# Attention and a feed-forward layer on one core: casts by two outer rows, w_out behind V of batch 1, matmuls in the set-up, and the global rows' store ahead of the last blocks

## The chip, the core and the metric

The kernel runs on one core of one Trainium2 chip. Time is device time in microseconds (us) of one launch of the kernel on that core. Five engines work at once: TensorE (PE; its loading of weights is listed as PEld), VectorE (DVE), ScalarE (ACT), GpSimd (POOL) and SyncE (SP). POOL and SP also issue transfers; a queue's name with a q behind it (POOLq, SPq) marks that in the rows of the timeline. Transfers are carried by 16 DMA engines, which all queues share.

## What is computed

```python
# attention: B, H, S, D = 8, 8, 576, 64; 8 global tokens
scores = (q @ k.T) / sqrt(D)
mask = (abs(pos[:, None] - pos[None, :]) <= 32) | is_global[:, None] | is_global[None, :]
x = softmax(where(mask, scores, -1e9)) @ v          # then (B*S, H*D) = 4608 x 512
# feed-forward
h = x @ w_in                                        # 512 x 2048
out = (h + sin(alpha * h)**2 / (alpha + 1e-9)) @ w_out   # 2048 x 512
```

All inputs are float32; the kernel's matmuls take bf16.

## The kernel before

**Stages.** The 8 batches go through the core one after the other, in two stages. `attention(b)` (L892 to L1026; `attention_first`, about L780 to L890, for batch 0) computes 576 tokens of 8 heads, two heads (`hp`) at a time: scores within windows (L929), the exponential on ACT (L938), the mask on DVE (L939), the products with V and with ones (L967), the reciprocal through a logarithm and an exponential on ACT (L771, L778), and the normalised result xT on DVE (L985). `gemm1(b)` (L1108 to L1165) multiplies xT by w_in in 16 groups `nt` of 128 columns (L1124) and makes H from each by a sine (L1154), a square (on ACT L1157 or DVE L1159) and one DVE operation (L1160). `gemm2(b)` (L1167 to L1190) multiplies H by w_out, in blocks of 128 tokens with 16 matmuls of 128x512 each (L1172), copies the result out of PSUM (L1182, the last block in two halves by ACT and DVE, L1180) and stores it (L1189, SP). It is a generator: `fill(n)` (L1216) takes the next n of its matmuls from a waiting list, so that they lie between the steps of the attention after it (after two heads each, by `FIRST` and `SECOND`; `NEAR` and `MIDST` at its end) and of gemm1 (`PER_GROUP`, `GROUP_LATE` in gemm1(1), `GROUP_LAST` in gemm1(7)). Rows of the 8 global tokens stand in 64 columns of their own; `gemm2_globals` (L1192 to L1211) multiplies those at the end of the kernel and scatters them into the output by POOL (L1208).

**How keys, queries and values come in.** For batches 1 to 7, POOL's queue casts k, q and v of a batch to bf16 from DRAM to DRAM (`cast_qk`, L332, buffers kd and qd; `cast_v`, L340, buffer vd; two buffers of each). SP then issues the transposing transfers kd to kt and qd to qt (`turn_qk`, L345), DVE copies these into the operands KX or KD and QX (`place`, L357 for queries, L364 for keys, eight copies a batch), and SP loads vd into VX or VD (`load_v`, L418), with the global rows of V beside it (`load_vg`, L422). For batch 0 the loads are direct (V at L397, by POOL). w_in comes in four parts of 512 columns (`load_w_in`, L430) and w_out in four parts (`load_w_out`, L436), cast by POOL's queue as well.

**What sets the order.** Every queue works in the order of the program. POOL's queue is held back by `pace` (L1241): a copy of one element that waits until the tile it reads is there, behind which the next transfers stand. In attention(0), POOL issues kd and qd of batch 1, waits by `pace` for kt of batch 1, and then issues parts 2 and 3 of w_in, vd of batch 1 and the four parts of w_out. In gemm1(0) at nt = 10 SP issues the global rows of V of batch 1; after gemm1(0) POOL issues kd and qd of batch 2. Ahead of gemm1(1) it waits by `pace` for qt of batch 2, and issues vd of batch 2 and kd, qd, vd of batch 3. From attention(2) on, `pace` waits for xT of the batch at its third pair of heads, and kd, qd, vd of the batch two further on follow. kt and qt of batch 2 are turned in attention(1), those of later batches after the gemm1 two batches earlier. The eight copies of `place` stand in gemm1(0) and gemm1(1) for batches 1 and 2 (nt 10 to 13), and in the attention before from batch 3 on: `places_at` puts two ahead of the first heads, one after the second pair, three after the third and two after the fifth step.

**The end.** gemm1(7) is followed by the blocks of gemm2(7) with the sums and squares of a check of the inputs' size (`square_x`, `square_w`, `judge_sums`, `judge`, L1043 to L1099) between them, then gemm2_globals. The verdict is read (L1314) and a branch (L1315) leads to a general path, which isn't taken here.

Of the kernel before, what the change touches and what calls it, by code (L numbers as in the profile page):

```python
# [10 lines left out]
ALU = mybir.AluOpType  # L11
AF = mybir.ActivationFunctionType
DT = mybir.dt
# [3 lines left out]
P = 128  # L17
# [232 lines left out]
def kernel(  # L250
# [65 lines left out]
    VG0 = main.tile([NG * B, D], DT.bfloat16, name="VG0")  # L316
    seen = main.tile([1, 1], DT.bfloat16, name="seen")
    girow = main.tile([1, NG], DT.int64, name="girow")
# [12 lines left out]
    def cast_qk(b):  # L331

        for src, name in ((k, "kd"), (q, "qd")):
            cast[b, name] = dramp.tile([P, H * S * D // P], DT.bfloat16, name=name)
            nc.gpsimd.dma_start(
                out=cast[b, name][:], in_=src[b].rearrange("h s d -> (h s d)").rearrange("(p f) -> p f", p=P)
            )

    def cast_v(b):

        cast[b, "vd"] = dramp.tile([S, H, D], DT.bfloat16, name="vd")
        nc.gpsimd.dma_start(out=cast[b, "vd"][:], in_=v[b].rearrange("h s d -> s h d"))

    def turn_qk(b):
# [304 lines left out]
    def place_global_queries(t, copy):  # L649
        for y in range(2):  # L650
# [246 lines left out]
    def attention(b, beside):  # L897
# [82 lines left out]
        def inverse(hp):  # L980
            Rs[hp] = inverted(Ls[hp])
# [124 lines left out]
    def gemm1(b):  # L1106
# [23 lines left out]
        for nt in range(NT):  # L1130
# [34 lines left out]


    def gemm2(b):  # L1167
        lo, hi = (0, 4) if b % 2 == 0 else (4, 9)
        for blk in range(lo, hi):
            ops = zo[(blk + b // 2) % 2]  # L1170
            for nt in range(NT):
                nc.tensor.matmul(  # L1172
                    out=ops[:], lhsT=H2[:, nt, blk * P : (blk + 1) * P], rhs=w_out[:, nt, :],
                    start=(nt == 0), stop=(nt == NT - 1),
                )
                yield True
            osb = osbp.tile([P, DM], DT.float32, name="osb")
            if b == B - 1 and blk == hi - 1:
                for e, copy in enumerate((nc.scalar.copy, nc.vector.tensor_copy)):
                    copy(out=osb[:, e * DM // 2 : (e + 1) * DM // 2], in_=ops[:, e * DM // 2 : (e + 1) * DM // 2])  # L1180
            else:
                nc.scalar.copy(out=osb[:], in_=ops[:])  # L1182

            c = blk * P
            while c < (blk + 1) * P:
                z = min((c // QTR + 1) * QTR, (blk + 1) * P)
                run, u = c // QTR, c % QTR
                t0 = (b // 2) * 2 * S + (run // 2) * HALF + run % 2 + 2 * u
                nc.sync.dma_start(  # L1189
                    out=out[t0 : t0 + 2 * (z - c) - 1 : 2, :], in_=osb[c - blk * P : z - blk * P, :]  # L1190
                )
                c = z  # L1192

# [45 lines left out]
    def pace(src):  # L1239

        nc.gpsimd.tensor_copy(out=seen[:], in_=src)  # L1241

    def phase_a(b_att, b_moe):
        def beside(at):

            if b_moe is None:
                if at == 0:
# [4 lines left out]
                    cast_v(1)  # L1252
                    load_w_out()
                    gather(v, gv)
# [27 lines left out]
    phase_a(0, None)  # L1282
    for b in range(B):
        if b == 1:
            pace(turned[2][0][0:1, 0:1])
            cast_v(2)
            cast_qk(3)
            cast_v(3)
# [6 lines left out]
        if b + 1 < B:  # L1295
# [16 lines left out]
    mctx.close()  # L1312

    sure = nc.values_load(verdict[0:1, 0:1], min_val=0, max_val=P)  # L1314
    with tc.If(sure < P):  # L1315
        general_path(tc, q, k, v, global_idx, out, w_in, w_out, alphaT, recipT)
# [30 lines left out]
```

## Time and profile before

| what | us |
|---|---|
| runs of the kernel before | 383.4, 383.32, 378.85 |
| their median | 383.32 |
| the profiled execution | 384.38 |
| its span, first to last instruction | 382.7 |
| set-up and attention(0), to | 31.4 |
| gemm1(0) | 31.4 to 54.5 |
| attention(1) | 54.5 to 82.4 |
| gemm1(1) | 82.4 to 107.0 |
| attention(2) | 107.0 to 126 |
| gemm1(2) | 126 to 147.8 |
| from then on, a batch about | 39 |
| gemm1(7) | 321 to 346 |

The profiled execution is one run with a hardware trace; its durations are what the prediction's sums are made of. Stages overlap at their edges, since matmuls of gemm2 lie in both. A row of the timeline has the start, the duration, the engine and line, the operation with what it writes and reads, a count, and in brackets how long the engine had been idle before it and which instruction ended that. A row of the waits has the engine, what it was about to write and its line, what it waited for, then the total, the number of waits and the longest. A row by windows has the window, its length, the busy time and count of PE, PEld, DVE, ACT and POOL, the granted TensorE clock as a share of full speed, the DMA share and GB/s. A row of a queue's transfers has the packets, the MB and the share of 16 engines' time that its packets took. A row of DMA issues has the buffers, the queue, the count, the KB of each and the median us from issue to landing.

### The profile page before, as it was taken

The numbers are of one execution on the slowest core, as the hardware profiler recorded it, in microseconds if no ns is written. First come the engines' busy times: TensorE is split into PE (matmuls) and PEld (weight loads), VectorE is DVE, ScalarE is ACT, GpSimd is POOL, SyncE is SP. The second block draws the span as 40 slices with busy tenths as digits, with TensorE's granted clock in tenths as the row PEclk, the third lists the DMA queues.
The fourth block names the chain that finished last, engine by engine and source line by source line (L and its number), as shares of the span: only waits on it lengthen the run. The fifth ranks groups of instructions, "written<-read, shape, count | busy, mean of one in ns | idle before, by whom it ended". The sixth has DMA issues, their size and how long they took to land. (4 is left out here: it accounts for less than half of the span.)

```text
span 382.7 us, 10443 instructions
## 1 busy us (share of the span) xinstructions
PE 323.6 (85%) x4222; PEld 206.1 (54%) x4280; DVE 275.5 (72%) x539; ACT 288.9 (75%) x425; POOL 55.1 (14%) x78
## 2 busy tenths in 40 slices
PE   2678753699988998899899989998998998899990
PEld 2566532356645664566556655665466655554440
DVE  6966897156969687967796788778877885889400
ACT  7879794278877888879887987898888886889110
POOL 7941730014004000400030002100000000000001
PEclk9999995599999999999999999999999999999996
DMA  7999999179994991395849693977232020002221
GB/s 121 117 162 170 184 207 224 27 153 153 203 196 80 208 183 30 69 189 100 149 81 163 119 153 86 146 155 123 59 93 51 0 58 32 3 0 83 64 75 49
DMA packets 91393, 43.23 MB, mean 113 GB/s; under 512 B 76394, under 2 KB 85994, under 8 KB 90890
## 3 DMA queue, kind: packets, MB, share of 16 engines
q0 software_dynamic: 44208, 18.52, 39.9%
q1 hardware_dynamic: 47130, 23.97, 30.2%
q8 instruction: 35, 0.57, 0.6%
q14 instruction: 20, 0.16, 0.1%
HBM read 41.97 MB, written 21.95 MB: 167 GB/s over the span
## 5 line engine op out<-in xcount | busy, mean ns | idle before, releaser
L1172 PE MATMUL zo<-w_out,H 128*128 128x512 bf16 x518 | 137.5, 382 | 4.6 <-issue 3.6
L1124 PEld LDWEIGHTS <-w_in 128*128 128x128 bf16 x1024 | 99.2, 98 | 53.0 <-issue 18.7
L1172 PEld LDWEIGHTS <-H 128*128 128x128 bf16 x576 | 51.0, 98 | 45.3 <-issue 0.7
L938 ACT ACTIVATE E<-ring 128x720 bf16<-128x720 f32 x56 | 43.3, 773 | 28.8 <-PE ring L929 28.8
L1124 PE MATMUL zn<-xT,w_in 128*128 128x288 bf16 (+1 forms) x384 | 57.0, 287 | 6.1 <-DVE H L1160 4.1
L1124 PE MATMUL zr<-xT,w_in 128*128 128x288 bf16 x320 | 47.7, 287 | 3.3 <-DVE H L1160 2.9
L1124 PE MATMUL zd<-xT,w_in 128*128 128x288 bf16 x320 | 46.3, 287 | 1.9 <-DMA w_in<-in_moe_w_in_dram 1.3
L1160 DVE SCALAR_TENSOR_TENSOR H<-s,recipT,zn 128x576 bf16<-128x576 bf16 (+1 forms) x48 | 39.4, 822 | 10.7 <-ACT s L1157 7.3
L1154 ACT ACTIVATE sb<-zn,alphaT 128x576 bf16<-128x576 f32 (+1 forms) x48 | 35.7, 743 | 14.6 <-PE zn L1124 13.5
L1157 ACT ACTIVATE s<-sb 128x576 bf16<-128x576 bf16 (+1 forms) x62 | 42.7, 689 | 2.0
L1159 DVE TENSOR_TENSOR s<-sb 128x576 bf16<-128x576 bf16 (+1 forms) x66 | 30.9, 468 | 14.2 <-ACT sb L1154 13.1
L939 DVE TENSOR_TENSOR E<-E,MASKT 128x720 bf16<-128x720 bf16 x56 | 29.2, 529 | 11.6 <-ACT E L938 11.1
L1160 DVE SCALAR_TENSOR_TENSOR H<-s,recipT,zd 128x576 bf16<-128x576 bf16 (+1 forms) x40 | 32.9, 822 | 6.4 <-ACT s L1157 4.3
L1160 DVE SCALAR_TENSOR_TENSOR H<-s,recipT,zr 128x576 bf16<-128x576 bf16 (+1 forms) x40 | 32.9, 822 | 5.9 <-ACT s L1157 3.4
L1154 ACT ACTIVATE sb<-zd,alphaT 128x576 bf16<-128x576 f32 (+1 forms) x40 | 29.6, 739 | 5.9 <-PE zd L1124 5.9
L1154 ACT ACTIVATE sb<-zr,alphaT 128x576 bf16<-128x576 f32 (+1 forms) x40 | 29.6, 741 | 3.5 <-PE zr L1124 3.4
L1182 ACT COPY osb<-zo 128x512 f32<-128x512 f32 x35 | 20.4, 582 | 14.2 <-PE zo L1172 14.1
L778 ACT ACTIVATE R<-L,shift 128x576 f32<-128x576 f32 x32 | 24.8, 774 | 0.6
L985 DVE TENSOR_TENSOR xT<-zn,R 128x576 bf16<-128x576 f32 x21 | 15.8, 754 | 8.8 <-PE zn L967 6.0
L1241 POOL COPY seen<-xT 1x1 bf16<-1x1 bf16 x4 | 1.9, 480 | 134.7 <-DVE GN L755 134.7
L1208 POOL DMA_INDIRECT out_dram<-osb,grow x1 | 1.0, 979 | 135.7 <-SPq L1315 135.7
L929 PEld LDWEIGHTS <-KX 64*64 64x64 bf16 x448 | 9.0, 111 | 20.9 <-issue 19.2
(169 smaller groups left out, 373.5 us busy)
## 6 DMA issues: line engine op xcount, KB each, us to landing
kd<-in_k_dram POOLq DMA_DIRECT2D x7, 576.0 KB, 6.5
qd<-in_q_dram POOLq DMA_DIRECT2D x7, 576.0 KB, 10.1
vd<-in_v_dram POOLq DMA_DIRECT2D x7, 576.0 KB, 15.4
VX<-vd SPq DMA_DIRECT2D x16, 168.0 KB
w_in<-in_moe_w_in_dram POOLq DMA_DIRECT2D x4, 512.0 KB, 5.8
w_out<-in_moe_w_out_dram POOLq DMA_DIRECT2D x4, 512.0 KB, 16.4
out_dram<-osb SPq DMA_DIRECT2D x8, 256.0 KB
VD<-vd SPq DMA_DIRECT2D x12, 168.0 KB
```

The lines of the kernel that those rows point to most:

```text
L778: nc.scalar.activation(out=R[:], in_=L[:], func=AF.Exp, scale=-1.0, bias=shift[:, 0:1])
L929: nc.tensor.matmul(out=zs[half * D : (half + 1) * D, t, 0 : G3 * WCOL].rearrange("p (m x c) -> p m x c", x=2, c=60)[:, m % G3, :, c0:c1], ...
L938: nc.scalar.activation(out=Eg, in_=zs[:, :, 0 : G3 * WCOL], func=AF.Exp, scale=scale)
L939: nc.vector.tensor_tensor(out=Eg, in0=Eg, in1=MASKT[:, None, G3 * g : G3 * (g + 1), :].rearrange("p o m c -> p o (m c)").to_broadcast([P, ...
L985: nc.vector.tensor_tensor(out=xT[:, hp, 0:S].rearrange("p (k m c) -> p k m c", k=4, c=KT), in0=tokens(nd(hp, 0)), in1=Rs[hp][:], op=ALU.mult,)
L1124: nc.tensor.matmul(out=h_part, lhsT=w_in[:, c, nt * P : (nt + 1) * P], rhs=xT[:, c, lo:hi], start=(c == 0), stop=(c == CT - 1), skip_group ...
L1154: nc.scalar.activation(out=sb[:, 0:W], in_=h, func=AF.Sin, scale=alphaT[:, nt : nt + 1])
L1157: nc.scalar.activation(out=s2[:, 0:W], in_=sb[:, 0:W], func=AF.Square)
L1159: nc.vector.tensor_tensor(out=s2[:, 0:W], in0=sb[:, 0:W], in1=sb[:, 0:W], op=ALU.mult)
L1160: nc.vector.scalar_tensor_tensor(out=H2[:, nt, r0 : r0 + W], in0=s2[:, 0:W], scalar=recipT[:, nt : nt + 1], in1=h, op0=ALU.mult, op1=ALU.add,)
L1172: nc.tensor.matmul(out=ops[:], lhsT=H2[:, nt, blk * P : (blk + 1) * P], rhs=w_out[:, nt, :], start=(nt == 0), stop=(nt == NT - 1),)
L1182: nc.scalar.copy(out=osb[:], in_=ops[:])
```

## The change

1. `cast_qk` views source and destination as two outer rows ("p (a c) -> a p c" with a = 2), each of 128 runs of 1,152 elements, where both were one contiguous list before.
2. `load_w_out` moves from attention(0) to gemm1(0), nt = 10, behind `load_vg(1)` and a new `pace` that reads 48 partitions of the second half of VX, the values of batch 1.
3. Twice seven matmuls whose result isn't used (`warm`) stand around the turning of keys and queries in the set-up.
4. At the end of an attention, `fill(NEAR)` stands ahead of the numerators of the last but one pair of heads.
5. `GROUP_LAST` takes 3 and then 13 times 1 matmul of gemm2(6) in gemm1(7), where it took 4 in all; 14 are left over there.
6. `gemm2_globals` and its scatter stand ahead of gemm2(7). For that, H of the global tokens of batch 7 is copied to its columns by eight POOL copies (`put_globals`, columns read from registers that `load_columns` fills at b = 2).
7. The last block of gemm2 is computed in two halves of 256 columns, each with its own copy by ACT and its own store.
8. The copies of `place` for batch 3 move to after the third pair (two) and after the fifth step (six) of attention(2).
9. The branch at the end has the general path as the one that is jumped to.

```diff
         for src, name in ((k, "kd"), (q, "qd")):
-            nc.gpsimd.dma_start(
-                out=cast[b, name][:], in_=src[b].rearrange("h s d -> (h s d)").rearrange("(p f) -> p f", p=P)
-            )
+            runs = [
+                t.rearrange("p (a c) -> a p c", a=2)
+                for t in (cast[b, name][:], src[b].rearrange("h s d -> (h s d)").rearrange("(p f) -> p f", p=P))
+            ]
+            nc.gpsimd.dma_start(out=runs[0], in_=runs[1])
...
+    warm(zo[0], 7)
     turn_part(1, 0, views([zn[:, n, :] for n in range(2)]))
...
     turn_part(0, 0, views([zd[:, n, :] for n in range(2)]))
+    warm(zo[0], 7)
...
         inverse(last - 1)
+        fill(NEAR)
         numerators(last - 1)
-        fill(NEAR)
...
                 load_vg(1)
+                pace(VX[1][D : D + KT, 0, 0, 0:1])
+                load_w_out()
...
+    def put_globals():
+        for j, c in enumerate(columns_of):
+            g = 2 * S + j * B + B - 1
+            nc.gpsimd.tensor_copy(out=H2[:, :, bass.ds(c, 1)], in_=H2[:, :, g : g + 1])
...
+            parts = 2 if (b, blk) == (B - 1, hi - 1) else 1
+            for part in range(parts):
+                cols = slice(part * DM // parts, (part + 1) * DM // parts)
+                if part:
+                    ops = zd[:, 1]
...
+                nc.scalar.copy(out=osb[:, cols], in_=ops[:, cols])
+                store(b, blk, osb, cols)
...
-    GROUP_LAST = (0, 0, 2) + 2 * (0, 0, 0, 1) + 5 * (0,)
+    GROUP_LAST = (0, 0, 3) + 13 * (1,)
...
-        share = {-1: (0, 2), 1: (2, 3), 2: (3, 6), 4: (6, 8)}
+        share = {2: (0, 2), 4: (2, 8)} if b_att == 2 else {-1: (0, 2), 1: (2, 3), 2: (3, 6), 4: (6, 8)}
...
                     load_w_in((2, 3))
                     cast_v(1)
-                    load_w_out()
...
-    waiting.append(gemm2(B - 1))
+    put_globals()
     square_x(B - 1, 0)
     square_x(B - 1, 1)
-    for c in range(CT):
+    square_w(0)
+    fill(NT)
+    square_w(1)
+    fill(4 * NT)
+    gemm2_globals()
+    judge_sums()
+    waiting.append(gemm2(B - 1))
+    for c in (2, 3):
         square_w(c)
         fill(NT)
-        if c == 1:
-            judge_sums()
     judge()
     fill(2 * NT * NT)
-    gemm2_globals()
...
-    with tc.If(sure < P):
+    with tc.If(sure < P, preferred_fallthrough_block=False):
```

On POOL, from the casts of batch 1 in attention(0) to those of batch 2 behind gemm1(0), the kernel before has these rows (a transfer's row has the shape of its destination, outermost dimension first; `seen` is what `pace` writes, KX, QX and VGb belong to batch 1):

```order
L335 DMA kd<-in_k_dram 32x9216
L335 DMA qd<-in_q_dram 32x9216
L1241 COPY seen<-kt 1x1
L430 DMA w_in<-in_moe_w_in_dram 128x4x512 x2
L342 DMA vd<-in_v_dram 4608x1x64
L436 DMA w_out<-in_moe_w_out_dram 128x4x512 x4
L1260 COPY MASKT<-MASK 64x720 x2
L719 CAST VGb<-H_97 64x512
L377 COPY KX_94<-kTg 128x48x8
L380 COPY QX_96<-qTg 128x4x7x4 x2
L335 DMA kd<-in_k_dram 32x9216
L335 DMA qd<-in_q_dram 32x9216
```

The changed kernel has these at the same place:

```order
L340 DMA kd<-in_k_dram 2x128x1152
L340 DMA qd<-in_q_dram 2x128x1152
L349 COPY seen<-kt 1x1
L437 DMA w_in<-in_moe_w_in_dram 128x4x512 x2
L345 DMA vd<-in_v_dram 4608x1x64
L1298 COPY MASKT<-MASK 64x720 x2
L728 CAST VGb<-H_97 64x512
L384 COPY KX_94<-kTg 128x48x8
L387 COPY QX_96<-qTg 128x4x7x4 x2
L349 COPY seen<-VX_93 48x1
L443 DMA w_out<-in_moe_w_out_dram 128x4x512 x4
L340 DMA kd<-in_k_dram 2x128x1152
```

w_out has moved from between vd of batch 1 and the copies of the mask to behind a second copy into `seen`, and stands directly ahead of kd and qd of batch 2; the casts' shape has changed.

On DVE, in attention(2), the copies of batch 3 (KX from kt, QX from qt) stand among the masks of the scores (E), the sums over the global tokens (GD, GN) and the results xT. Before, the piece from the first of them to the one behind the third pair of heads reads:

```order
L364 COPY KX_94<-kt 64x48x24 x2
L939 TENSOR_TENSOR E<-E,MASKT 128x2x360 x2
L1053 TENSOR_TENSOR SQ<-xT 128x4x576
L939 TENSOR_TENSOR E<-E,MASKT 128x2x360 x2
L755 TENSOR_REDUCE GD<-zd 128x2x4
```

And after the change, the piece with the first two of them:

```order
L948 TENSOR_TENSOR E<-E,MASKT 128x2x360
L764 TENSOR_REDUCE GD<-zd 128x2x4
L371 COPY KX_94<-kt 64x48x24 x2
L948 TENSOR_TENSOR E<-E,MASKT 128x2x360
L994 TENSOR_TENSOR xT<-zn,R 128x576
```

The two copies have moved from ahead of the first mask of attention(2) to behind the second GD, where a single copy of KX stood before; the six others follow together behind the last GN of that attention.

On POOL, at the end of the program, the kernel before has these rows (the last casts, the scatter, the reading of the verdict):

```order
L1241 COPY seen<-xT 1x1
L335 DMA kd<-in_k_dram 32x9216
L335 DMA qd<-in_q_dram 32x9216
L342 DMA vd<-in_v_dram 4608x1x64
L1208 DMA out_dram<-osb,grow 4608x512
L1314 TENSOR_LOAD verdict
L1315 COMPARE_AND_BRANCH
```

The changed kernel's end, from the last of the eight copies on:

```order
L1205 ISA
L1205 COPY H_97<-H_97 128x16
L1251 DMA out_dram<-osb,grow 4608x512
L1358 TENSOR_LOAD verdict
L1359 COMPARE_AND_BRANCH
```

The scatter now stands behind eight copies of H to H (128 partitions, 16 elements) and is followed by the same reading of the verdict; in the program it comes ahead of gemm2(7).

More of the change, by code (lines that the diff above doesn't have):

```diff
@@ L316 @@
     VG0 = main.tile([NG * B, D], DT.bfloat16, name="VG0")
-    seen = main.tile([1, 1], DT.bfloat16, name="seen")
+    seen = main.tile([P, 1], DT.bfloat16, name="seen")
+    gcol = main.tile([1, NG], DT.int32, name="gcol")
     girow = main.tile([1, NG], DT.int64, name="girow")
@@ L342, in cast_v, with pace @@
         nc.gpsimd.dma_start(out=cast[b, "vd"][:], in_=v[b].rearrange("h s d -> s h d"))
+    def pace(src):
+        nc.gpsimd.tensor_copy(out=seen[0 : src.shape[0]], in_=src)
     def turn_qk(b):
@@ L1170, in gemm2, with store @@
             ops = zo[(blk + b // 2) % 2]
[L1171 to L1176, printed above, removed]
-            osb = osbp.tile([P, DM], DT.float32, name="osb")
[L1178 to L1192, printed above, removed]
+            osb = osbp.tile([P, DM], DT.float32, name="osb")
+            parts = 2 if (b, blk) == (B - 1, hi - 1) else 1
[3 more added lines that the diff above has]
+                    ops = zd[:, 1]
+                for nt in range(NT):
+                    nc.tensor.matmul(
+                        out=ops[:, cols], lhsT=H2[:, nt, blk * P : (blk + 1) * P], rhs=w_out[:, nt, cols],
+                        start=(nt == 0), stop=(nt == NT - 1), skip_group_check=True,
+                    )
+                    yield True
+                nc.scalar.copy(out=osb[:, cols], in_=ops[:, cols])
+                store(b, blk, osb, cols)
+    def store(b, blk, osb, cols):
+        c = blk * P
+        while c < (blk + 1) * P:
+            z = min((c // QTR + 1) * QTR, (blk + 1) * P)
+            run, u = c // QTR, c % QTR
+            t0 = (b // 2) * 2 * S + (run // 2) * HALF + run % 2 + 2 * u
+            nc.sync.dma_start(
+                out=out[t0 : t0 + 2 * (z - c) - 1 : 2, cols], in_=osb[c - blk * P : z - blk * P, cols]
+            )
+            c = z
     def gemm2_globals():
```

23 lines of the change are left out of this document (21 added, 2 removed).

## The prediction, on record before the changed kernel ran

> **What bounds the kernel now.** I read the header of the page and its clock row first, then the waits by engine, the timeline of the first 120 us, the transfers of a few windows, and the tail.
>
> ```profile
> PE 323.6 (85%) x4222; PEld 206.1 (54%) x4280; DVE 275.5 (72%) x539; ACT 288.9 (75%) x425; POOL 55.1 (14%) x78
> PEclk9999995599999999999999999999999999999996
> 60.00:70.00 10.00, 2.18 (x44) 1.10 (x36) 5.49 (x16) 2.75 (x4) 0.00 (x0) 0.50 0.80 172
> 70.00:80.00 10.00, 8.84 (x195) 5.10 (x198) 3.86 (x10) 4.89 (x8) 0.00 (x0) 0.68 0.42 75
> PE zn L967 <- DMA VX<-VGb: 7.2, 2, 4.8
> PE zd L1124 <- DMA w_in<-in_moe_w_in_dram: 1.3, 1, 1.3
> ```
>
> TensorE is the busiest engine (85%) and no single wait is large. One place in the middle is weak: around 60 to 80 us PE is nearly empty, and the granted clock, 0.9 or more elsewhere, is 0.50 and 0.68 (the last two numbers but two of the window rows). The wait that ends there is for V of batch 1: 7.2 us in two pieces. The other wait, for the second half of w_in, is only 1.3 us, and it is on this row that the change bears hardest. The timeline shows the chain of POOL's queue, of SP's queue and of PE behind both (start, us, what, and in brackets the idle time before):
>
> ```profile
> 23.15 0.55 POOL L335 DMA_DIRECT2D kd<-in_k_dram  x1
> 36.65 0.18 POOL L1241 COPY seen<-kt 1x1 bf16<-1x1 bf16 x1 [12.44 <-DMA kt<-kd]
> 36.88 1.54 POOL L430 DMA_DIRECT2D w_in<-in_moe_w_in_dram  x2
> 38.41 2.26 POOL L342 DMA_DIRECT2D vd<-in_v_dram  x1
> 40.12 3.53 POOL L436 DMA_DIRECT2D w_out<-in_moe_w_out_dram  x4
> 29.60 4.68 SPq L348 DMA_TRANSPOSE kt<-kd  x1
> 51.60 1.63 SPq L418 DMA_DIRECT2D VX<-vd  x4
> 42.85 1.15 PE L1124 MATMUL zd<-xT,w_in 128*128 128x288 bf16 x8 [1.33 <-DMA w_in<-in_moe_w_in_dram]
> 67.89 0.28 PE L967 MATMUL zn<-E,VX 56*64 56x88 bf16 x2 [4.82 <-DMA VX<-VGb]
> 70.56 0.78 PE L967 MATMUL zn<-E,VX 56*64 56x88 bf16 x26 [2.39 <-DMA VX<-VGb]
> ```
>
> The reader is to see a chain without slack: cast of the keys, transpose kt, the paced POOL copy, w_in, PE at 42.85. Whatever the cast takes longer, PE gets late w_in.
>
> **The casts.** Each cast was one list of 32 rows of 9,216 elements; now its outermost dimension is 2, with 128 runs of 1,152 inside. The whole question is over how many of the 16 DMA engines two outer rows are spread.
>
> ```profile
> q0 software_dynamic: 81, 0.90, 74.5%
> q0 software_dynamic: 681, 0.68, 73.6%
> q0 software_dynamic: 44208, 18.52, 39.9%
> VD<-in_v_dram POOLq DMA_DIRECT2D x16, 36.0 KB, 4.9
> ```
>
> The first row is the window 26.4 to 32.1 us, where nearly all bytes are those of the casts: 0.745 x 16 x 5.7 = 67.9 us of engine time for 0.90 MB. Its long packets have 18,432 bytes, and 0.90 MB is 49 of them: 1.386 us for one, so 32 x 1.386 = 44.4 us for a cast, 2.8 us if 16 engines share it, 22.2 us on two. The second row is the window 36.9 to 43 us, whose packets have 1 KB: 0.736 x 16 x 6.1 / 681 = 0.105 us each. A run of 1,152 bf16 has 2,304 bytes. On the line between the two rows it takes 0.202 us, and a cast 256 x 0.202 / 2 = 25.7 us on two engines; at the rate of the 1 KB packets it would be 30 us. I take 25.7 with ends 22.2 and 30.
>
> Two engines or sixteen? The third row (the whole page) lets the packets be counted. Transfers of POOL's queue have, by their shapes, 41,824 runs of data, and 53 transfers with 16 closing writes each give 848: 42,672. The row has 44,208, which is 1,536 or 16 x 96 more. There are exactly 16 transfers whose outer dimension isn't a multiple of 16: the loads of V (fourth row), 24 rows of 12 runs. 96 is 4 x 24: as if 12 engines took two rows (24 runs) each, and 4 idle ones wrote 24 empty entries each. So the spread goes by the outer dimension (12 divides 24) and not by all runs (288 divides by 16). Two rows then give two engines. The casts' own rows show only an outer dimension of 32 and say nothing of fewer, so an even split stays a rival. The Trainium skill, page "DMA: Bandwidth & Descriptors", section "Rules for kernel authors", speaks against this change: an outermost dimension of fewer than 16 confines a transfer to at most that many engines. By that rule the sum below holds; by the even spread that the casts' rows show it would be the first rival's. No run so far shows a transfer with two rows.
>
> **Costs, step by step.** I follow the sum against the profiled execution: 384.38 us for a span of 382.7, 1.1 us over the median of 383.32 (runs 378.85 to 383.4).
>
> *First cast, +23.9 (20.4 to 28.2).* kt(1) comes 25.7 − 2.8 = 22.9 us later, POOL's copy behind it and w_in too; PE waits at nt = 8 of gemm1(0), where it is 1.3 us late already, so nothing hides it. Behind so long a wait I add 1 us for matmuls at half clock (8.84 us of PE work at 0.68 in the window above lost about 2.8 us; this wait is followed by less). SP's queue has only stores of no hurry behind kt.
>
> *V of batch 1 and w_out, −8.5 (−10 to −7.2).* w_out's four transfers no longer stand in the rings ahead of the V loads; vd goes right behind w_in. The two waits of 4.82 and 2.39 us go, and part of the slow clock (1.3 us of the 2.8). w_out now waits on POOL for V: V landed is about 75, w_out issued 76 to 80 and landed by 96. It is first used at the end of attention(1), which the first cast pushes back as well, so I cost that at nothing here.
>
> *Second casts, +12 (5 to 18).* kd(2) and qd(2), issued ahead of V until now, stand behind w_out's packets on their engines.
>
> ```profile
> 75.18 2.21 SPq L348 DMA_TRANSPOSE kt<-kd  x1
> 99.18 0.92 DVE L364 COPY KD<-kt 64x1152 bf16<-64x1152 bf16 x2
> 83.97 0.18 POOL L1241 COPY seen<-qt 1x1 bf16<-1x1 bf16 x1 [30.65 <-DMA qt<-qd]
> 86.69 1.04 POOL L335 DMA_DIRECT2D kd<-in_k_dram  x1
> 103.44 5.32 SPq L348 DMA_TRANSPOSE kt<-kd  x1
> 111.68 0.92 DVE L364 COPY KX<-kt 64x1152 bf16<-64x1152 bf16 x2 [3.29 <-DMA kt<-kd]
> 119.99 0.46 DVE L364 COPY KX<-kt 64x1152 bf16<-64x1152 bf16 x1
> q0 software_dynamic: 4134, 0.53, 140.7%
> q0 software_dynamic: 939, 1.29, 106.2%
> ```
>
> They start when w_out is through, about 96.5, land at 122, and kt(2) is turned at 126.7 (4.7 us, as kt(1)). The copy at 99.18 wants it at 99.18 + 23.9 − 8.5 = 114.6: 12 us. The ends are a w_out that lands 7 us earlier or 6 later.
>
> *Third casts, +24 (14 to 30).* POOL's copy at 83.97 waits for qt(2), now turned at 128.5. vd(2) and kd(3) are queued behind it: the last two rows are the windows 86 to 91.9 us, in which POOL's rings moved nothing but vd's short runs, and 91.9 to 98.7 us, with kd's and qd's bytes. So kd starts 8 us after the copy, now runs from 136.5 to 162, and kt(3) is there at 167 (5.32 us). The copies of batch 3 that stood at 111.68 now stand where the row of 119.99 does, ahead of which go 3.29 us of waiting and 1.37 us of copies: they want kt(3) at 115.3 + 27.4 (the sum so far) = 143. The move takes the 3.29 us away only if kt(3) is on time.
>
> *Batches 4 to 7, +10 (0 to 25).*
>
> ```profile
> 159.24 0.72 POOL L335 DMA_DIRECT2D kd<-in_k_dram  x1
> 183.55 3.06 SPq L348 DMA_TRANSPOSE kt<-kd  x1
> 190.14 0.92 DVE L364 COPY KX<-kt 64x1152 bf16<-64x1152 bf16 x2 [1.48 <-DMA kt<-kd]
> ```
>
> From issue to the first use are 188.7 − 159.2 = 29.5 us. The cast needs 1.4 us to start, 25.7 to run, and the transposes 5: 32, or 2.5 us too late, four times. With 22.2 it fits; with 30 it is 6 a batch.
>
> *Tail, −4 (−5 to −1).*
>
> ```profile
> 372.06 1.94 PE L1200 MATMUL zd<-w_out,H 128*64 128x256 bf16 x32
> 372.21 0.37 ACT L1180 COPY osb<-zo 128x256 f32<-128x256 f32 x1 [2.87 <-PE zo L1172]
> 374.08 0.37 ACT L1207 COPY osb<-zd 64x256 f32<-64x256 f32 x1 [1.50 <-PE zd L1200]
> 376.59 0.98 POOL L1208 DMA_INDIRECT out_dram<-osb,grow x1 [135.74 <-SPq L1315]
> SPq L1342 <- DMA out_dram<-osb,grow: 5.3, 1, 5.3
> ```
>
> The last product was that of the global rows: 1.94 us of matmuls, two copies, a scatter issued at 376.59 and 5.3 us of waiting for it. Done ahead of gemm2(7), the scatter lies beside some 20 us of matmuls. After the change the last block ends the kernel, whose second half is 1.5 us of matmuls and a 0.37 us copy, with a store behind it as long as the scatter at worst. So about 10.9 us from 372.06 to the end become 7. Eight POOL copies that place the global columns stand ahead of it; by the 0.18 us of a one-element copy they are 1.4 us or more, beside matmuls that gemm1(7) leaves over (14 instead of none), 14 x 0.38 = 5.3 us of them. Were that cover gone, they cost up to 3.
>
> *Small things, −1 (−2.6 to +1).* fill(NEAR) ahead of the numerators covers waits of PE for the reciprocal; twice seven spare matmuls in the set-up are 14 x 0.38 = 5.3 us of PE in a stage that waits for data, hidden if the products of V or the transposes don't wait for them.
>
> Sum: 23.9 − 8.5 + 12 + 24 + 10 − 4 − 1 = +56.4, so 440.8 against 384.38, and 440 against the median. All low ends together give 406, all high ends 478.
>
> **The rivals.**
> *The casts still use all 16 engines.* Then the runs are shorter and no later. For it: the casts' packets are now spread evenly. Against: the count of empty entries. Then −8.5, w_out 1.5 late, −4, −1: 384.4 − 12 = 372, or 371 to the median. This is the one that ends faster, decided by whether two rows give 16 engines.
> *Only the first cast hurts.* Later ones could hide: the 30.65 us that POOL waited for qt(2) show how early everything was issued. Against it: the 3.29 and 1.48 us by which kt was late with quick casts. 384.4 + 23.9 − 8.5 − 4 − 1 = 395, or 394.
> *Both casts share one pair of engines.* Then qd lands 25.7 us behind kd: attention(1) waits for its queries, some 25 us more, the third casts as much again, and each later batch about 10 where the queries' copies come 10 us behind the keys': 440 + 25 + 25 + 40 = 530. Nothing in the rows tells pairs apart.
>
> **How the numbers follow.** Two engines each on pairs of their own: 0.73. All 16: 0.13. Only the first: 0.07. One pair: 0.07. The time is the first's, 440. Its own range is 406 to 478; with the case of 394 taken in, and some room above since the lateness of one batch could add to the next, 392 to 485 leaves out the first and third rival, 0.20. A measurement of this kernel tells about 2% from no change. Faster by more is the rival of 371: 0.13. Within 2% needs a mixture near the edge, such as a cast better hidden than the second rival: 0.04. Slower is the rest, 0.83.
>
> **What would show it.** A kd packet train of about 25 us in place of 5; the wait for w_in at L1124 at about 24 us instead of 1.3; waits for kt on DVE at two later places of 12 and 24 us; no wait for VX. If w_in is on time, the spread is even and the forecast falls at its first step; if it is late but DVE never waits for kt(3), the third step was wrong. The tail should end with a store and no scatter.

## The result, and the profile after

The changed kernel takes 495.49 us (median of 4 runs, 494.24 to 497.68) against 383.12 us before: a ratio of 1.297, with a 95% interval of 1.287 to 1.308. The forecast was 440 with a range of 392 to 485. The way was right, the time was too small by 55 us. Times here and below are medians of all runs, while a ratio compares only the runs outside a second, slower state that some executions fall into, so it can differ a little from the quotient of the two times. The profiled execution of the changed kernel took 495.08 us, its span is 493.4.

The header of its page, its clock row and POOL's rings:

```profile
PE 353.3 (72%) x4310; PEld 217.1 (44%) x4310; DVE 285.6 (58%) x545; ACT 289.2 (59%) x426; POOL 66.7 (14%) x87
PEclk9998576898887655669999979996999799999999
q0 software_dynamic: 72432, 18.62, 39.4%
kd<-in_k_dram POOLq DMA_DIRECT2D x7, 576.0 KB, 32.2
```

The work of DVE and ACT is nearly what it was. PE's row went up by 30 us, but about 22 us of that are 58 matmuls of gemm2 (at 0.38 us) that the trace of before has no records of: it lists 518 and 576 of their weight loads. Most of the rest are the spare matmuls, and matmuls at a lower clock. What grew is idle time. A cast now lands 32.2 us after its issue (median), 6.5 before. The packets of POOL's rings went from 44,208 to 72,432, 28,224 more. 14 casts of 256 runs in place of 32 rows make 3,136; the rest is 25,088 = 14 x 14 x 128: for each cast, as if 14 engines wrote 128 empty entries each. Packets under 512 bytes, by the same page, went up by nearly as many, from 76,394 to 101,498. That bears out the count on which the prediction's two engines rested.

The last sine of each gemm1 marks the stages. These rows are the ACT timeline of the kernel before, for batches 0, 1, 2 and 7:

```profile
54.11 0.74 ACT L1154 ACTIVATE sb<-zn,alphaT 128x576 bf16<-128x576 f32 x1 [0.16 <-PE zn L1124]
106.24 0.74 ACT L1154 ACTIVATE sb<-zn,alphaT 128x576 bf16<-128x576 f32 x1 [0.17 <-DVE H L1160]
147.03 0.72 ACT L1154 ACTIVATE sb<-zn,alphaT 128x576 bf16<-128x576 f32 x1
343.62 0.78 ACT L1154 ACTIVATE sb<-zn,alphaT 128x640 bf16<-128x640 f32 x1
```

And these the same four of the changed kernel:

```profile
75.85 0.72 ACT L1165 ACTIVATE sb<-zn,alphaT 128x576 bf16<-128x576 f32 x1
130.21 0.74 ACT L1165 ACTIVATE sb<-zn,alphaT 128x576 bf16<-128x576 f32 x1 [4.43 <-PE zn L1133]
233.28 0.72 ACT L1165 ACTIVATE sb<-zn,alphaT 128x576 bf16<-128x576 f32 x1
458.83 0.78 ACT L1165 ACTIVATE sb<-zn,alphaT 128x640 bf16<-128x640 f32 x1
```

Differences of such rows give a table of stages in us; each is from one last sine to the next, of one profiled execution. Single traces scatter here: a kernel below that differs from before only in its end has 55.3, 50.4 and 42.9 us for the first three, so a difference of 2 us in a stage says nothing.

| stage | before | changed | more | forecast |
|---|---|---|---|---|
| to the end of gemm1(0) | 54.1 | 75.9 | +21.7 | +23.9 |
| attention(1), gemm1(1) | 52.1 | 54.4 | +2.2 | −8.5 + 12 |
| attention(2), gemm1(2) | 40.8 | 103.1 | +62.3 | +24 |
| batches 3 to 6 and attention(7), gemm1(7) | 196.6 | 225.6 | +29.0 | +10 |
| behind the last sine | 39.1 | 34.6 | −4.5 | −4 |

Three of the five are near the forecast. One is 38 us worse, one 19. The chain of the first stage reads as it was drawn (SP, POOL and PE; start, us, what, idle before):

```profile
51.49 2.10 SPq L355 DMA_TRANSPOSE kt<-kd  x1
55.87 0.18 POOL L349 COPY seen<-kt 1x1 bf16<-1x1 bf16 x1 [29.86 <-DMA kt<-kd]
62.26 2.10 PE L1133 MATMUL zd<-xT,w_in 128*128 128x288 bf16 x8 [19.40 <-DMA w_in<-in_moe_w_in_dram]
```

kt is issued 21.9 us later than before (51.49 against 29.60), and PE goes on 19.4 us later (62.26 against 42.85). While nothing but the first two casts ran, POOL's rings took this share of 16 engines, in the window 28.3 to 51.4 us:

```profile
q0 software_dynamic: 1871, 1.15, 28.9%
```

A quarter would be four engines, kd and qd on two each; one pair for both would be an eighth, with the empty entries on top in either case. The third rival falls.

In attention(2) DVE waits for kt and then for qt of batch 3. The timeline of POOL, SP and DVE around it, from the casts of batch 3 to the copies of its queries:

```profile
123.55 1.58 POOL L340 DMA_DIRECT2D qd<-in_q_dram  x1
154.63 1.06 POOL L340 DMA_DIRECT2D kd<-in_k_dram  x1 [0.49 <-issue]
155.68 1.07 POOL L340 DMA_DIRECT2D qd<-in_q_dram  x1
155.32 16.66 SPq L355 DMA_TRANSPOSE kt<-kd  x1
172.15 26.58 SPq L355 DMA_TRANSPOSE qt<-qd  x1
188.25 0.92 DVE L371 COPY KX<-kt 64x1152 bf16<-64x1152 bf16 x2 [32.49 <-DMA kt<-kd]
211.16 1.86 DVE L364 COPY QX<-qt 64x1152 bf16<-64x1152 bf16 x4 [13.91 <-DMA qt<-qd]
```

kd of batch 3 is down at 155.3, earlier than the 162 that I had forecast. But its transpose, 5.3 us before, is only usable at 188, and that of the queries at 211. The casts of batch 4, keys and queries by the rows above and values at 156.73, were issued at the very moment when the transposes began. Two windows of the SP queue's transfers show what happened, 51.4 to 57 us (transposes of batch 1, no cast beside them) and 155.4 to 172 us:

```profile
q1 hardware_dynamic: 4345, 1.10, 89.3%
q1 hardware_dynamic: 1372, 0.35, 86.3%
```

0.893 x 16 x 5.6 / 4345 = 18.4 ns for one packet of the transpose alone, and 0.863 x 16 x 16.6 / 1372 = 167 ns beside the casts, near the 0.202 us that I had put for one packet of a cast. The queue moves one packet where it moved nine.

The waits for kt and qt are not all of this stage. PE stands idle three times in it; the rows are the landing of a store of results (from the chain of work that ended last: start, us, what), ACT's copy that waited for it, and PE's three:

```profile
132.73 16.18 DMA out_dram<-osb
149.01 0.59 ACT L1223 COPY osb<-zo 128x512 f32<-128x512 f32 x1 [11.91 <-DMA out_dram<-osb]
150.32 0.51 PE L938 MATMUL ring<-QX,KD 64*64 64x88 bf16 x14 [11.08 <-ACT E L947]
190.59 0.79 PE L976 MATMUL zn<-E,VD 56*64 56x88 bf16 x28 [31.18 <-DVE GN L764]
215.70 2.08 PE L1133 MATMUL zn<-xT,w_in 128*128 128x288 bf16 x8 [16.34 <-DVE H L1171]
```

Together these are 58.6 of the 62.3 us. The last two are DVE's waits for kt and for qt. The first comes ahead of them and has another cause: ACT can't reuse the buffer of a store that takes 16.18 us to land while the casts of batch 3, issued from 122.5 on, move beside it. In the kernel before, none of the four computing engines waits longer than 0.2 us for a store.

### The profile page after: what moved, and what is told of

Same layout as the page of the kernel before. It is cut to its first block, busy times and chain, and to the rows that moved or that the text cites. A ratio compares the mean times of both kernels' runs of the same rounds, so it can differ in the third digit from the quotient of the medians.

```text
span 493.4 us, 10613 instructions
## 1 busy us (share of the span) xinstructions
PE 353.3 (72%) x4310; PEld 217.1 (44%) x4310; DVE 285.6 (58%) x545; ACT 289.2 (59%) x426; POOL 66.7 (14%) x87
## 3 DMA queue, kind: packets, MB, share of 16 engines
q0 software_dynamic: 72432, 18.62, 39.4%
## 4 chain that ended last, share of the span: by engine, by line
DMA 44%; PE 30%; DVE 9%; ACT 7%; SPq 4%; issue 3%; POOL 2%; DVEq 0%; ACTq 0%; POOLq 0%
DMA kd<-in_k_dram 18%; PE zo L1218 14%; DMA qt<-qd 9%; DMA kt<-kd 6%; PE zn L1133 5%; SPq L355 4%; DMA out_dram<-osb 3%; PE zr L1133 3%; DVE H L1171 3%; ACT sb L1165 3%; PE zd L1133 2%; DMA VD<-vd 2%; DMA H<-in_q_dram 2%; PE ring L938 2%; PE zd L976 1%
## 5 line engine op out<-in xcount | busy, mean ns | idle before, releaser
L1218 PE MATMUL zo<-w_out,H 128*128 128x512 bf16 (+1 forms) x576 | 158.8, 398 | 0.0
L1133 PEld LDWEIGHTS <-w_in 128*128 128x128 bf16 x1024 | 101.2, 100 | 97.1 <-issue 41.9
L1133 PE MATMUL zn<-xT,w_in 128*128 128x288 bf16 (+1 forms) x384 | 58.9, 294 | 24.7 <-DVE H L1171 23.0
L1218 PEld LDWEIGHTS <-H 128*128 128x128 bf16 x592 | 54.6, 101 | 48.7 <-issue 7.6
L1133 PE MATMUL zd<-xT,w_in 128*128 128x288 bf16 x320 | 47.3, 292 | 19.8 <-DMA w_in<-in_moe_w_in_dram 19.4
L947 ACT ACTIVATE E<-ring 128x720 bf16<-128x720 f32 x56 | 43.3, 773 | 28.1 <-PE ring L938 27.9
L1133 PE MATMUL zr<-xT,w_in 128*128 128x288 bf16 x320 | 49.8, 296 | 7.3 <-DVE H L1171 7.0
L1171 DVE SCALAR_TENSOR_TENSOR H<-s,recipT,zn 128x576 bf16<-128x576 bf16 (+1 forms) x48 | 39.4, 822 | 13.6 <-ACT s L1168 10.3
L1223 ACT COPY osb<-zo 128x512 f32<-128x512 f32 (+1 forms) x36 | 20.7, 575 | 38.0 <-DMA out_dram<-osb 24.4
L371 DVE COPY KX<-kt 64x1152 bf16<-64x1152 bf16 (+1 forms) x20 | 8.4, 421 | 50.7 <-DMA kt<-kd 50.4
L364 DVE COPY QX<-qt 64x1152 bf16<-64x1152 bf16 (+1 forms) x32 | 23.4, 730 | 14.5 <-DMA qt<-qd 13.9
L780 ACT ACTIVATE L<-zd 128x576 f32<-128x576 f32 x24 | 15.5, 647 | 21.5 <-PE zd L976 21.5
L976 PE MATMUL zn<-E,VD 56*64 56x120 bf16 (+2 forms) x252 | 5.4, 234 | 31.4 <-DVE GN L764 31.4
## 6 DMA issues: line engine op xcount, KB each, us to landing
kd<-in_k_dram POOLq DMA_DIRECT2D x7, 576.0 KB, 32.2
```

What stands on the lines that cost most here:

```text
L364: copy(out=QX[b % 2][rows, hps, y, PAD : PAD + 6 * SEG].rearrange("p h (m c) -> p h m c", c=SEG)[:, :, :, 4:], in_=src.rearrange("p h (m a ...
L780: nc.scalar.activation(out=L[:], in_=den, func=AF.Ln, scale=2.0**-SHIFT)
L947: nc.scalar.activation(out=Eg, in_=zs[:, :, 0 : G3 * WCOL], func=AF.Exp, scale=scale)
L1133: nc.tensor.matmul(out=h_part, lhsT=w_in[:, c, nt * P : (nt + 1) * P], rhs=xT[:, c, lo:hi], start=(c == 0), stop=(c == CT - 1), skip_group ...
L1171: nc.vector.scalar_tensor_tensor(out=H2[:, nt, r0 : r0 + W], in0=s2[:, 0:W], scalar=recipT[:, nt : nt + 1], in1=h, op0=ALU.mult, op1=ALU.add,)
L1218: nc.tensor.matmul(out=ops[:, cols], lhsT=H2[:, nt, blk * P : (blk + 1) * P], rhs=w_out[:, nt, cols], start=(nt == 0), stop=(nt == NT - 1) ...
```

## The experiments

The rivals after the result: theory A, the two outer rows are the whole loss; theory B, the move of w_out or the copies have a large share; theory C, short runs are slow by themselves; theory D, the transposes of batch 3 share engines with the casts of batch 4, against theory E, the cast simply lands that late.

**The changed kernel with the casts as one list again.**

```diff
-            nc.gpsimd.dma_start(out=runs[0], in_=runs[1])
+            nc.gpsimd.dma_start(
+                out=cast[b, name][:], in_=src[b].rearrange("h s d -> (h s d)").rearrange("(p f) -> p f", p=P)
+            )
```

> The changed kernel with the casts of keys and queries as one list of 32 rows again, all else as changed. Theory A (two outer rows put a cast on two DMA engines, and that is the whole loss): the wait for w_in at gemm1(0) goes from 19.4 us back to about 1 to 2, no wait of DVE for kt over 4 us, and the time is the 371 us of the first rival, 368 to 376. Theory B (moving w_out behind V, so that the casts of batch 2 stand behind it, or the new tail has a large share in the loss): 390 us or more.

It took 379.67 us, ratio 0.988 (0.983 to 0.994). The loss is gone, PE waits 1.4 us for w_in and DVE 1.4 us for kt, and no computing engine waits for a store in mid-kernel. Theory A holds: the time is over its 368 to 376, but the runs that the ratio compares have a median of 376.0.

**Only the two outer rows, in the kernel before.** The edit is the change's first hunk alone.

> The kernel before with the casts in two outer rows as the only edit. Theory A: each cast takes 24 to 31 us; the wait for w_in is 18 to 20 us, V of batch 1 still waits behind w_out, and attention(2) and gemm1(2) grow by tens of us; in all 480 to 515. If the move of w_out or of the copies of batch 3 were needed for the long stage around attention(2) (theory B), it is 420 to 450.

466.57 us, ratio 1.224 (1.214 to 1.235), between the two forecasts and within neither. It loses 84 us where the whole change loses 112, and its stages tell where most of the other 28 come from: attention(2) with gemm1(2) takes 64.9 us (129.4 to 194.3), 24 more than before and not 62. This kernel keeps the copies of batch 3 ahead of the first heads there. So the outer rows explain most, but 38 us of that stage need another part of the change as well, which e1 alone could not show.

**The same short runs in 16 outer rows.**

```diff
-                t.rearrange("p (a c) -> a p c", a=2)
-                for t in (cast[b, name][:], src[b].rearrange("h s d -> (h s d)").rearrange("(p f) -> p f", p=P))
+                t.rearrange("(y x c) -> x y c", x=16, y=16)
+                for t in (cast[b, name][:].rearrange("p f -> (p f)"), src[b].rearrange("h s d -> (h s d)"))
```

> The changed kernel with the casts in the same runs of 1,152 elements, but 16 outer rows of 16 runs each (the runs go in another order; the same bytes move). Theory A (the outer dimension sets the engines): a cast takes 16 x 0.191 = 3.1 us, the packets are of the same 2,304 bytes, and the time is that of the kernel with whole casts within 2%, about 371. Theory C (runs of 2,304 bytes are slow by themselves): the time stays above 450.

376.98 us, ratio 0.990 (0.986 to 0.995). The packets of this kernel, and the landing of its casts:

```profile
q0 software_dynamic: 47344, 18.52, 42.0%
kd<-in_k_dram POOLq DMA_DIRECT2D x7, 576.0 KB, 7.4
```

47,344 is 44,208 − 448 + 14 x 256: the runs are the short ones and there is no empty entry more. Landing is 7.4 us against 32.2. Theory C falls: runs of 2,304 bytes cost nothing that shows in the time, and the whole loss goes with the outer dimension.

**The casts of batch 4 held back.** Still two outer rows; in attention(2) `pace` waits for qt of batch 3.

```diff
-                pace(xTs[b_att][0:1, 0, 0:1])
+                pace(turned[3][0][0:1, 0:1] if b_att == 2 else xTs[b_att][0:1, 0, 0:1])
```

> The changed kernel, casts still in two outer rows; in attention(2) the casts of batch 4 wait for qt of batch 3 instead of for xT of batch 2. Theory D (in attention(2) the transposes of batch 3 run beside the casts of batch 4, and on the four engines of those their packets take turns one by one, which makes 33 and 39 us of 5): kt of batch 3 is there 5 us after kd, attention(2) with gemm1(2) grows by some 25 us instead of 62, and the time falls to 455 to 470 unless the later casts of batch 4 give it back in gemm1(3), in which case 470 to 485. Theory E (kd of batch 3 simply lands that late): the time stays at 490 or more.

461.88 us, ratio 1.212 (1.204 to 1.220), 34 us less than the changed kernel by an edit that makes casts later. The transpose and the first copy in attention(2):

```profile
166.80 1.06 POOL L340 DMA_DIRECT2D kd<-in_k_dram  x1 [0.49 <-issue]
164.26 0.92 DVE L371 COPY KX<-kt 64x1152 bf16<-64x1152 bf16 x2 [8.33 <-DMA kt<-kd]
```

The copy runs at 164.3 where it ran at 188.3, with a cast that isn't in the way. The stage takes 64.1 us (131.4 to 195.5), 23 more than before. Theory E falls, theory D holds. The edit holds back all three casts of batch 4, so by itself it doesn't tell the share of keys and queries from that of the values.

**The copies of batch 3 back at their old places.** Still two outer rows.

```diff
-        share = {2: (0, 2), 4: (2, 8)} if b_att == 2 else {-1: (0, 2), 1: (2, 3), 2: (3, 6), 4: (6, 8)}
+        share = {-1: (0, 2), 1: (2, 3), 2: (3, 6), 4: (6, 8)}
```

> The changed kernel, casts in two outer rows, with the DVE copies of batch 3 back at their old places in attention(2) (two ahead of the first heads). Theory D (the copies moved behind the issue of the casts of batch 4, so that kt and qt of batch 3 share four engines with these casts): with the copies ahead, DVE holds attention(2) until kt is there, the casts of batch 4 are issued after it, kt takes about 5 us again, attention(2) with gemm1(2) takes 63 to 66 us instead of 103, and the time is 455 to 470, like that of the kernel that holds those casts back. Theory F (the long stage comes from the queue's order w_out, kd, qd, and the copies' place doesn't matter): 485 or more.

469.9 us, ratio 1.238 (1.218 to 1.258). The first copy waits 29.0 us and holds attention(2); the casts of batch 4 are issued behind it:

```profile
161.52 0.92 DVE L371 COPY KX<-kt 64x1152 bf16<-64x1152 bf16 x2 [29.02 <-DMA kt<-kd]
169.89 1.06 POOL L340 DMA_DIRECT2D kd<-in_k_dram  x1 [0.49 <-issue]
```

The stage takes 69.5 us, somewhat more than forecast, against 103.1. So the pair is shown from both sides: the move of the copies put the wait for kt behind the issue of the next casts. Before, DVE's wait for kt stood ahead of the xT for which `pace` waits, and kept the casts of batch 4 away from the transposes without any line that says so.

**Four outer rows.** The edit is a=4 for a=2.

> The changed kernel with four outer rows of 128 runs of 576 elements. Theory A (the outer dimension is the number of engines): a cast takes 128 packets of about 0.106 us on each of four engines, 13.6 us; the wait for w_in is 8 to 11 us; the later casts fit their 30 us (13.6 + 6 of others' packets + 2 + 6 for the transposes), so that the steady batches cost nothing; 384 to 400 in all. If small runs cost more than their bytes (theory C) or the four engines collide: 410 or more.

398.84 us, ratio 1.051 (1.035 to 1.067). PE waits 9.9 us for w_in; batches 3 to 6 take 39.0, 39.6, 38.5 and 40.4 us, hardly more than before (39.4, 39.2, 38.9, 39.1). All forecasts met, the total at the upper edge: attention(2) with gemm1(2) still takes 53.0 us, 12 more than before, and ACT waits 9.6 us for a store there. kd lands in 19.3 us (median): the steady batches have slack for that and not for 32. The count of packets, 72,432 again, is 44,208 − 448 + 14 x (512 + 12 x 128), the count for four engines with data and 12 without.

**Sixteen outer rows without the spare matmuls.** Two lines `warm(zo[0], 7)` less.

> The kernel with 16 outer rows, without the 14 spare matmuls of the set-up. Theory G (they bring on the 10 us of half clock between 17 and 27 us, which the kernel before doesn't have, and gemm1(0) ends later for it): the first sine is 1 us earlier and the time 1 to 2 us less, 374 to 376. Theory H (they are free or a gain): 377 or more.

375.93 us, ratio 0.992 (0.987 to 0.996), against 0.990 (0.986 to 0.995) with them. The granted clock around 18 to 26 us, which is 1.00 in the kernel before and without the spare matmuls, is 0.50 with them in the 16-row kernel (first two rows). But the changed kernel with two outer rows has the same matmuls and 1.00 there (third row):

```profile
18.00:22.00 4.00, 1.51 (x16) 1.13 (x14) 3.87 (x10) 3.73 (x9) 1.96 (x3) 0.50 1.32 97
22.00:26.00 4.00, 3.74 (x37) 3.22 (x38) 2.49 (x7) 2.57 (x5) 3.20 (x6) 0.50 1.10 146
22.00:26.00 4.00, 3.82 (x37) 3.26 (x37) 3.37 (x10) 3.50 (x7) 4.00 (x5) 1.00 1.29 152
```

Of the six traces with these matmuls three have such a stretch, of the eight without them none: they may bring it on, as theory G has it, but not every time. The first sine comes at 34.1 without and 34.3 us with them, the last one of gemm1(0) at 54.5 and 57.4, and that of gemm1(2) at 146.6 and 144.6, the other way round. The intervals overlap widely: the two theories are not told apart in time, and the matmuls brought nothing that can be measured.

**Only the move of w_out, in the kernel before.** The hunks with `load_w_out` and the new `pace`.

> The kernel before with w_out's move behind V of batch 1 as the only edit. By the prediction's second step: no wait for V in attention(1), which with gemm1(1) gets 7 to 9 us shorter, and the time 374 to 376. By the rival that this gain is given back in gemm1(0) and attention(2) (later casts of batch 2, copies that come late): 378 to 383.

387.41 us, ratio 1.021 (1.010 to 1.033): slower by 1 to 3%, beyond both forecasts. attention(1) with gemm1(1) gets 5.5 us shorter (46.6 against 52.1), with no wait for V. But the first copy of batch 3 then waits longer:

```profile
112.72 0.92 DVE L364 COPY KX<-kt 64x1152 bf16<-64x1152 bf16 x2 [9.90 <-DMA kt<-kd]
```

It waited 3.29 us before. The chain w_out, kd, qt, `pace`, vd, kd to kt of batch 3 ends where it did (kt issued at 102.0, before at 103.4), so DVE is merely there earlier, and attention(2) with gemm1(2) takes 49.9 us, 9 more.

**Only the changed end, in the kernel before.** The scatter ahead, eight POOL copies, the last block in halves, the fills of gemm1(7), the branch.

> The kernel before with the changed end alone: global columns placed by POOL, global rows multiplied and scattered ahead of gemm2(7), the last block in two halves, the fills of gemm1(7) and the branch as changed; casts, w_out, set-up and copies as before. By the prediction's sixth step: 4 us less than before, ratio 0.985 to 0.997, the gain behind the last sine (39.1 us there before, 34 to 35 now). If the end gains nothing by itself: ratio 0.997 to 1.005.

379.06 us, ratio 0.995 (0.991 to 1.000). Behind the last sine there are 34.6 us against 39.1 in the profiled executions, as forecast; the ratio of whole runs shows about half of it, with an interval that reaches to no gain.

**w_out and the copies of batch 3 moved together, in the kernel before.**

> The kernel before with w_out behind V of batch 1 and the copies of batch 3 at their new places, nothing else. Theory I (w_out's move makes attention(1) 5.5 us shorter, and the copies ahead of attention(2) gave all of it back in a wait for kt of batch 3 of 9.9 us; the later copies find kt there): the wait of DVE for kt falls under 3 us, attention(2) with gemm1(2) is back at 41 to 46 us, and the time is 376 to 381. Rival: the wait only moves to the later place and the time stays at 385 or more.

382.37 us, ratio 1.005 (1.002 to 1.008). The wait for kt is 2.2 us and the stage 43.1 us, as theory I has it, but the total is 1 us over its range. In this trace gemm1(0) ends 1.7 us later than before, which is within the scatter of single traces. The copies' move undoes what w_out's move cost; the two together gain nothing.

**Keys of batch 3 ahead of values of batch 2.** With 16 outer rows, without the spare matmuls.

```diff
-            cast_v(2)
             cast_qk(3)
+            cast_v(2)
```

> The changed kernel with 16 outer rows and without the spare matmuls, and with kd and qd of batch 3 issued ahead of vd of batch 2. By theory I the last wait for kt of batch 3 (1.5 us) goes and kt is turned some 4 us earlier: 374 to 376, ratio to the kernel before 0.978 to 0.992. If V of batch 2 comes late instead, a wait for VD shows in attention(2) and the time is 377 or more.

373.82 us, ratio 0.983 (0.977 to 0.988): the fastest of all. The first copy of batch 3 waits for nothing, and attention(2) with gemm1(2) takes 40.6 us, where the kernel with 16 rows and no spare matmuls took 45.7:

```profile
112.12 0.91 DVE L371 COPY KX<-kt 64x1152 bf16<-64x1152 bf16 x2
```

What w_out's move gave in attention(1) is no longer given back there. In whole runs the order of the two casts is worth about 2 us of that (373.82 against 375.93), in runs that were not taken side by side and with intervals that just touch.

**Only fill(NEAR) ahead of the numerators, in the kernel before.**

> The kernel before with fill(NEAR) ahead of the numerators of the last but one pair of heads, nothing else. From the traces so far: batches 3 to 6 take 38.5 to 38.8 us from last sine to last sine with it and 38.9 to 39.3 without. If the fill does that, these batches are 0.3 to 0.5 us shorter here too and the time 1.5 to 3 us less, 378 to 381, ratio 0.990 to 0.998. If it doesn't (the gain is of the shorter runs or of the end), they stay at 38.9 to 39.3 and the ratio is within 0.997 to 1.004.

382.82 us (4 runs, 375.39 to 384.25) against 381.63 for the kernel before beside it (7 runs, 380.13 to 384.3): too scattered for a ratio, so the time stays open. In its trace batches 3 to 6 take 38.9 us each on average (146.9 to 302.4), before 39.2 (147.0 to 303.7). A gain of 0.3 us a batch is in line with this, and not shown.

## Why the prediction was right in its way and wrong in its size

*Two engines for two rows.* Right, and with it the direction: undone, the loss is gone (0.988), with 16 rows too (0.990), and the empty entries are counted. The first rival, an even spread, fell. Had the casts been spread, its 371 would also have been too hopeful by 5 to 6 us (376.0 and 377.0 were measured), for a reason below. (One size in that step is off without effect: between its two rows a run of 2,304 bytes comes to 0.200 us, not 0.202.)

*First cast, +23.9.* Measured +21.7: kt was issued 21.9 us later, PE came 19.4 us later, and the first eight matmuls behind the wait took 2.10 us where they took 1.15. Right.

*V of batch 1 and second casts, −8.5 and +12.* Together +2.2 for a forecast +3.5, partly by luck. No wait for V is left. The wait for kt of batch 2 was 5 us and not 12, since w_out lands in 7.9 us now (16.4 before) when no V is beside it. But a pair of query copies then took 6.60 us, one of them 6.1 us where the longest before took 0.75, while POOL issued the casts behind its pace; no run tests why:

```profile
118.04 0.92 DVE L371 COPY KD<-kt 64x1152 bf16<-64x1152 bf16 x2 [5.24 <-DMA kt<-kd]
121.53 6.60 DVE L364 COPY QX<-qt 64x1152 bf16<-64x1152 bf16 x2
```

*Third casts, +24.* This is the step that failed. "kd runs from 136.5 to 162 and kt(3) is there at 167 (5.32 us)": the first half was near (155.3), the second wrong. The 5.32 us are the time in which SP's queue issued that transpose; kt was usable 8.2 us after 103.44 (3.29 us of wait, ended at 111.68). And they come from a trace in which no cast of keys or queries was on the engines beside it, only one of values. From 103.4 to 111.7 us in the kernel before, SP's and POOL's queues moved

```profile
q1 hardware_dynamic: 3303, 1.07, 89.6%
q0 software_dynamic: 2408, 0.31, 57.7%
```

which is 0.896 x 16 x 8.3 / 3303 = 36 ns for a packet of SP's queue, twice the 18.4 alone and far from 167. In the changed kernel the casts of keys and queries of batch 4 were there too, since the copies of batch 3 had been moved behind their issue. I had looked at that move for the 3.29 us it could save, and not for what the wait that it moved had held back until then. With the casts held back, or the copies at their old place, the stage grows by 23 and 29 us, and by 24 with the outer rows alone. The other 38 are the contention of transposes and casts: with the casts held back, PE's second and third idle piece are 7.0 and 2.5 us, and in the changed kernel they are 31.2 and 16.3.

That 23 is so near the forecast's 24 is luck. With the copies at their old place DVE does wait 24.2 and 29.0 us for kt, but at the new place, which the forecast priced, it waits only 8.33 us with the casts held back. Half of the 23 is a wait that stood in no term of mine, that of ACT for the store of results:

```profile
149.34 0.59 ACT L1223 COPY osb<-zo 128x512 f32<-128x512 f32 x1 [11.61 <-DMA out_dram<-osb]
```

It is most of why, in the changed kernel, the copies want kt(3) at 155.8 (188.25 − 32.49) and not at 143. Such a wait of 7.7 to 11.9 us shows in each kernel with two outer rows, one of 9.6 with four, and none with casts on all engines.

*Batches 4 to 7, +10.* The term was mis-sized: 29 us, where 2.5 us four times became 7 to 12 us three times; DVE's three waits for kt there make 28.1 us. The chain of work that ended last reads, for one of them:

```profile
245.71 32.23 DMA kd<-in_k_dram
277.99 7.71 DMA kt<-kd
```

From issue to first use the forecast had 1.4 + 25.7 + 5 = 32 us. Measured are 32.2 + 7.7 = 40. The cast's packets shared their engines with other transfers, which would account for the difference to the first cast; no run changes only that. The SP queue's share of 16 engines in the window 27.3 to 51.4 us (first cast) and in 247.5 to 277.9 us (this one) was

```profile
q1 hardware_dynamic: 432, 0.10, 3.2%
q1 hardware_dynamic: 1301, 1.57, 18.4%
```

0.184 x 30.4 = 5.6 us an engine against 0.8 us: the loads of V and the output's stores. And the transposes ran beside the rest of vd, which lands 35.8 us after its issue. My bound of 25 us for this term held the short runs' rate open, but not other packets.

*Tail, −4.* Measured −4.5 behind the last sine, here and in the kernel with the changed end alone.

*w_out's gain without the outer rows.* The −8.5 of the first rival was worth 5.5 us in attention(1), and by itself it ended as a loss (1.021), since the next chain, kt of batch 3, was late at once. That wait, 3.29 us, stood in the rows of before, and I had used it only for the third casts.

What stays open: whether fill(NEAR) gains; why one copy of queries took 6.1 us; whether the casts of keys and queries slow the transposes without those of values beside them; and by what rule a transpose's packets all slow down.

## What to carry to other kernels

A transfer's duration from a trace holds for the traffic that was beside it there: when a change makes one transfer long, look up which others will now meet it, stores of results among them, and price those again. A wait can keep two transfers apart without being meant to; before an instruction that waits is moved, ask what is queued behind it on its own engine and on those that wait for its result. And look at the outermost dimension of a transfer before its run length: here 2, 4 and 16 outer rows of the same bytes were worth 495, 399 and 377 us.

## What the runs showed of the hardware

- A cast from DRAM to DRAM with two outer rows used two DMA engines: 28.9% of 16 engines busy with two casts in flight, and a count of packets that fits 128 empty entries from each of the 14 others. With four outer rows the count fits four engines, and the median landing was 19.3 us where it was 32.2.
- Packets of a DMA transpose took 18.4 ns alone, 36 ns (with some of other transfers) beside a cast of values in short runs, and 167 ns beside that and casts of keys and queries in two outer rows. Such transposes were usable 4.3 us after their issue alone, 8.2 us beside values, and 33 and 39 us beside all three.
- A store of results took 16.2 us to land beside casts in two outer rows; the longest waits of a computing engine for a store were 7.7 to 12.5 us in every kernel with such casts, and 0.2 us at most in the kernel before.
- Casts in runs of 2,304 bytes over 16 outer rows landed in 6.8 to 7.4 us (medians), those in 32 rows of 18,432 bytes in 6.4 to 7.2: the run length made no difference that shows.
- 14 spare matmuls in the set-up went with a granted clock of 0.50 from 18 to 26 us in three of six traces; in the eight traces without them it was 1.00.
